# A transformer block on one core: the mixer's second stage reads the input and normalises it again, and some transfers and vector steps change their slots

## The chip, the cores and the metric

The kernel runs on one core of a Trainium2 chip. The core has a matrix engine (TensorE, PE in the profile; its weight loads are listed apart as PEld), a vector engine (VectorE, DVE), a scalar engine for functions such as the exponential (ScalarE, ACT), a general engine (GpSimd, POOL) and a sync engine (SyncE, SP), which here only issues transfers. Each engine runs its own instructions in its own order and waits for the others at semaphores. Transfers are issued by SP and POOL and carried out by 16 DMA engines. Matrix products are written to PSUM, which DVE and ACT can read; everything else lies in SBUF or in DRAM.

The metric is the device time of one execution in microseconds, and of several executions the median.

## The reference

All inputs are bfloat16. The sequence has 2048 tokens of 512 values.

```python
x  = A_x                                   # [1, 2048, 512]
xn = layernorm(x)                          # over the 512 values
# A: attention, 32 heads of 128, with given keys and values
q  = (xn @ A_wq) split into 32 heads
p  = softmax(q @ k_cache^T * 128 ** -0.5)  # 2048 x 2048 for each head
s  = concat(p @ v_cache) @ A_wo
# B: a mixer on the same xn, which it normalises once more
h  = gelu(layernorm(xn) @ B_w1)            # 512 x 512
hs = (h, its four quarters shifted by 1, -1, 2, -2 tokens) @ B_w2
x1 = xn + hs
h2 = gelu(layernorm(x1) @ B_w3) @ B_w4     # 512 x 1792, 1792 x 512
out = x + s * silu(x1 + h2)
```

The largest part of the work is attention: for each head 2048 x 2048 scores, their exponentials, and their product with the values.

## The kernel before

Attention is cut into 128 units. A unit is one head with a block of 512 query tokens; units run by groups of four heads, in a group by query block, in a block by head. A unit has 8 slots (`SPU`), so the main loop has 1024 slots; slot n is slot p = n % 8 of unit u = n // 8. In each slot PE multiplies two key chunks with the queries (`s_slot`, tile `ps_s`), and ACT takes the exponential of the 128x1024 result into `pT`. Five slots later (`LAG`) PE multiplies `pT` with the values (`pv_slot`, tile `ps_o`). DVE adds the exponentials up in `acc` (`add_first`, `add_next`, `add_last`), PE turns them into sums over the keys (`sums`, `ps_sum`, in slot 3 of the next unit), DVE takes the reciprocal `rc`, and SP sends it through DRAM (`dr`) to all partitions (`rb`). In slot 2 of the unit after that, `norm` multiplies `ps_o` by `rb` into `oT`, which frees one of the two `ps_o` buffers; the unit that comes two later writes into it from its slot 5.

The queries of unit u + 2 are made in slots 0 and 1 of unit u (`q_mm`, `ps_q`), from the transposed normalised input `xnT` and the head's weights, and copied by DVE in slot 2 (`q_copy`, `qT`). The first unit of each query block of the first group needs four new tiles of tokens in `xnT`: unit 4 (made in slots 22 and 23) tiles 4 to 7, unit 8 (slots 48 and 49) tiles 8 to 11, unit 12 (slots 80 and 81) tiles 12 to 15. The queries, the sums and the output projection share one PSUM tile by turns.

The output projection (`wo_mm`, `wo_post`) and the mixer (`chunks`: `m1_chunk`, `m2_chunk`, `m3_chunk`, `m4_chunk`, tiles `ps_m`) run as additional matrix work inside the slots, the mixer in slots 2, 3, 6 and 7 at an even density from unit 5 on. The mixer's second stage `m2_chunk(t)` works on token tile t: four products in `ps_m`, then `x1` on DVE, which adds the normalised input from the tile `xr` and so frees `ps_m`, then new statistics (`stats`). Since layernorm of an already normalised row is almost the same row, the mixer's first layernorm is the same `xn`.

The 2048 tokens are 16 tiles of 128. For each tile, `ln1_load` brings the input (`xin`), `ln1_stats` takes mean and variance on DVE (`bn`, `mv`) and the reciprocal root on POOL (`rsqrt`: `ve`, `rs`), `ln1_apply` normalises it on DVE into `xn`, has SP transpose it into `xnT` by a DMA, and has POOL write `xn` to DRAM (`xn_d`). The tiles 0 to 3 go another way (`first_tokens`, transposed by PE), but are written to `xn_d` too, in slots 9 to 12. `xn_load(t)` reads `xn_d` back for the mixer's second stage.

The order on each engine is the program order wherever `pin(...)` stands, and nearly everything is pinned. `at(n, fn)` puts a step behind the fixed work of slot n. SP and POOL issue their transfers one after the other, so that a transfer whose data are not ready holds up those behind it. For the token tiles 4 to 15 the slots of `ln1_stats` and `ln1_apply` are two lists in one loop; `ln1_load` of the tiles 8 to 15 comes 8 slots ahead of the statistics.

At the end, `tail_open` in unit 121 (`QUIET`) loads what the last four token tiles need, `gate_sum(t)` prepares their result on DVE with two operations on 128x512 tiles, in slot 4 of units 122 to 125, and behind the loop stands the drain: the last products of unit 127, its sums and reciprocal, `norm`, and the last projections.

Of the kernel before, what the change touches and what calls it, by code (L numbers as in the profile page):

```python
# [17 lines left out]
def kernel(  # L18
# [15 lines left out]
    nc = tc.nc  # L34
# [4 lines left out]
    Sq, D = x2d.shape  # L39
# [91 lines left out]
    def at(n, fn):  # L131
        todo[n].append(fn)
# [213 lines left out]
    def ln1_stats(t):  # L346
        xin = ln[t]
        bn = smp.tile([P, nc.vector.BN_STATS_DIM], FP32, name="bn")
        mv = smp.tile([P, nc.vector.BN_AGGR_DIM], FP32, name="mv")
        rs = smp.tile([P, 1], FP32, name="rs")  # L350
        pin(nc.vector.bn_stats(out=bn[:], in_=xin[:]))  # L351
        pin(nc.vector.bn_aggr(out=mv[:], in_=bn[:]))
        rsqrt(rs[:], mv[:, 1:2])
        ln[t] = (xin, mv, rs)

    def ln1_norm(t):
        xin, mv, rs = ln.pop(t)
        xn = tokp.tile([P, D], BF16, tag="tb", bufs=8, name="xn")
        pin(nc.vector.tensor_scalar(
            out=xn[:], in0=xin[:], scalar1=mv[:, 0:1], scalar2=rs[:],  # L360
            op0=ALU.subtract, op1=ALU.mult))
        return xn

    def ln1_apply(t):
        xn = ln1_norm(t)
        pin(nc.sync.dma_start_transpose(out=xnT[:, :, t * P:(t + 1) * P], in_=xn[:]))
        pin(nc.gpsimd.dma_start(out=xn_d[t][:], in_=xn[:]))

# [5 lines left out]
    def first_tokens():  # L374
# [453 lines left out]
```

## Time and profile before

| what | value |
|---|---|
| median of 3 executions | 1293.24 us |
| lowest, highest | 1289.54, 1295.29 us |
| the profiled execution, device time | 1290.41 us |
| its span, first to last instruction | 1288.6 us |
| PE, ACT, DVE, POOL busy | 1267.2, 1114.5, 1016.6, 146.0 us |
| PE's mean granted clock | 0.997 |
| DMA, mean over the span | 88 GB/s |

Lines of the timelines give the start, the length, the engine, the line of the kernel, the operation, the tile written and those read, and the count; in brackets stands how long the engine had been idle before it, and what the profile names as the releaser. PE's instructions all have line 115, the helper `mm`, so they are told apart by tile. SPq is SP's queue of transfers; its entries are the issue of a transfer, not its run. A row "DMA to landing" gives the least, the middle and the greatest time from the issue to the arrival of the data. Granted clock 1.00 is PE's full speed.

### The profile page before, as it was taken

Reading aid. Unit: us, or ns where it says so; the run is one execution under the profiler, and the core shown is the slowest. Engines: PE = TensorE matmul, PEld = TensorE weight load, DVE = VectorE, ACT = ScalarE, POOL = GpSimd, SP = SyncE. Lnnn points to the kernel's source line nnn. Section 1 sums busy time; section 2 is a strip of 40 time slices with the busy share of each in tenths; the row PEclk is TensorE's granted clock in tenths of the full one; section 3 lists DMA queues with packets and bytes.
Section 4 is the critical chain, followed back from the end, with each engine's and each line's share of the span. In section 5 each row is a group of like instructions: output and inputs, shape, how many; then the busy total and the mean of one; then the engine's idle time right before and its main releaser. Section 6 shows DMA issues by size and latency. Waiting matters only on the chain.

```text
span 1288.6 us, 17369 instructions
## 1 busy us (share of the span) xinstructions
PE 1267.2 (98%) x6320; PEld 612.3 (48%) x6320; DVE 1016.6 (79%) x1392; ACT 1114.5 (86%) x1195; POOL 146.0 (11%) x257
## 2 busy tenths in 40 slices
PE   8899999999999999999999999999999999999998
PEld 4444444444444444444444444444444444444443
DVE  6887788888788777778787777888777888777895
ACT  7788998888999988899998889998888999888983
POOL 5332002333111110000001000000000000000110
PEclk9999999999999999999999999999999999999999
DMA  9644353357433553234344234523635134452521
GB/s 185 148 96 104 70 89 84 80 121 153 103 74 79 98 112 82 58 74 79 71 91 89 58 78 84 100 51 66 100 73 99 33 68 73 90 107 54 138 68 54
DMA packets 173718, 113.89 MB, mean 88 GB/s; under 512 B 125056, under 2 KB 150144, under 8 KB 173632
## 3 DMA queue, kind: packets, MB, share of 16 engines
q1 hardware_dynamic: 163904, 85.51, 33.9%
q0 software_dynamic: 9440, 27.01, 8.3%
q8 instruction: 49, 0.80, 0.3%
q14 instruction: 37, 0.30, 0.1%
q10 hardware_dynamic: 288, 0.26, 0.1%
HBM read 82.58 MB, written 9.70 MB: 72 GB/s over the span
## 4 chain that ended last, share of the span: by engine, by line
PE 85%; ACT 7%; DVE 5%; DMA 1%; issue 1%; POOL 0%; DVEq 0%; SPq 0%; ACTq 0%; POOLq 0%
PE ps_s L115 31%; PE ps_o L115 29%; PE ps_m L115 9%; PE ps_wo L115 8%; PE ps_q L115 7%; ACT pT L195 5%; DVE acc L206 2%; PE ps_sum L115 1%; ACT sq L431 1%; DMA xin<-in_A_x_dram 1%; ACT pre L461 1%; DVE acc L211 1%; DMA vb<-in_A_v_cache_dram 0%; DVE bn L351 0%; DVE qT L181 0%
## 5 line engine op out<-in xcount | busy, mean ns | idle before, releaser
L195 ACT ACTIVATE pT<-ps_s 128x1024 bf16<-128x1024 f32 x1024 | 1013.4, 1030 | 148.9 <-PE ps_s L115 145.1
L115 PE MATMUL ps_s<-qT,kT 128*128 128x512 bf16 x2048 | 609.6, 379 | 2.0 <-ACT pT L195 0.7
L115 PE MATMUL ps_o<-pT,vb 128*128 128x512 bf16 x2048 | 609.1, 379 | 2.1 <-DVE oT L262 2.1
L206 DVE TENSOR_TENSOR acc<-acc,pT 128x2048 bf16<-128x2048 bf16 x254 | 309.9, 1220 | 59.8 <-ACT pT L195 54.2
L115 PEld LDWEIGHTS <-kT 128*128 128x128 bf16 x2048 | 226.9, 113 | 224.6 <-issue 19.1
L115 PEld LDWEIGHTS <-vb 128*128 128x128 bf16 x2048 | 200.0, 98 | 228.0 <-issue 3.4
L201 DVE TENSOR_TENSOR acc<-pT 128x2048 bf16<-128x2048 bf16 x128 | 155.8, 1217 | 30.9 <-ACT pT L195 30.7
L115 PE MATMUL ps_q<-xnT,wq_h 128*128 128x512 bf16 (+1 forms) x524 | 152.4, 375 | 5.5 <-DVE acc L211 2.6
L115 PE MATMUL ps_wo<-wo_h,oT 128*128 128x512 bf16 x468 | 138.8, 379 | 0.0
L329 DVE TENSOR_TENSOR s_acc<-ps_wo,s_acc 128x512 f32<-128x512 f32 x100 | 68.9, 689 | 81.8 <-PE ps_wo L115 81.8
L262 DVE TENSOR_TENSOR oT<-ps_o,rb 128x512 bf16<-128x512 f32 x129 | 87.2, 676 | 6.1 <-DMA rb<-dr 6.1
L211 DVE TENSOR_TENSOR acc<-acc 128x1024 bf16<-128x1024 bf16 x127 | 87.9, 692 | 4.3
L181 DVE CAST qT<-ps_q 128x512 bf16<-128x512 f32 x122 | 83.6, 685 | 9.7 <-PE ps_q L115 9.7
L115 PEld LDWEIGHTS <-wq_h 128*128 128x128 bf16 x524 | 50.6, 98 | 66.6 <-issue 6.4
L115 PEld LDWEIGHTS <-oT 128*128 128x128 bf16 x480 | 46.9, 98 | 57.7 <-issue 2.6
L115 PE MATMUL ps_m<-xn2T,w_sb 128*128 128x512 bf16 x224 | 66.5, 378 | 0.0
L115 PE MATMUL ps_m<-w_sb,h2T 128*128 128x512 bf16 x224 | 63.9, 378 | 0.0
L580 POOL DMA_DIRECT2D w_sb<-in_B_w_dram x28 | 21.1, 755 | 352.7 <-PE ps_m L115 317.2
L212 DVE TENSOR_TENSOR acc<-acc 128x512 bf16<-128x512 bf16 x127 | 54.0, 425 | 4.3
L115 PEld LDWEIGHTS <-acc 128*128 128x128 bf16 x516 | 37.0, 115 | 33.9 <-DVE acc L212 5.9
L234 DVE RECIPROCAL rc<-ps_sum 128x4 f32<-128x4 f32 x128 | 22.9, 179 | 37.1 <-PE ps_sum L115 36.1
L612 POOL DMA_DIRECT2D g_d<-xr x16 | 8.8, 548 | 345.3 <-DVE xr L610 345.3
(75 smaller groups left out, 604.1 us busy)
## 6 DMA issues: line engine op xcount, KB each, us to landing
rb<-dr SPq DMA_DIRECT2D x128, 256.0 KB, 4.4
vb<-in_A_v_cache_dram SPq DMA_DIRECT2D x64, 256.0 KB, 4.6
w_sb<-in_B_w_dram POOLq DMA_DIRECT2D x28, 256.0 KB, 4.2
wo_h<-in_A_wo_dram SPq DMA_DIRECT2D x32, 128.0 KB, 4.5
wq_h<-in_A_wq_dram SPq DMA_DIRECT2D x28, 128.0 KB, 4.8
kT<-in_A_k_cache_dram SPq DMA_TRANSPOSE x128, 4.7
xn_d<-xn POOLq DMA_DIRECT2D x16, 128.0 KB, 4.1
dr<-rc SPq DMA_DIRECT2D x128, 2.0 KB, 1.4
```

Of the source, the lines that this page charges most:

```text
L115: pin(nc.tensor.matmul(out=out, lhsT=lhsT, rhs=rhs, start=start, stop=stop))
L181: pin(nc.vector.tensor_copy(out=qT[:], in_=st[u].pop("psq")[:]))
L195: pin(nc.scalar.activation(out=s["pT"][-1][:, jj:jj + 2, :], in_=sps[:], func=ACT.Exp, scale=SCALE))
L201: pin(nc.vector.tensor_tensor(out=s["acc"][:], in0=s["pT"][0][:], in1=s["pT"][1][:], op=ALU.add))
L206: pin(nc.vector.tensor_tensor(out=a[:], in0=a[:], in1=st[u]["pT"][i][:], op=ALU.add))
L211: pin(nc.vector.tensor_tensor(out=a[:, 0:2, :], in0=a[:, 0:2, :], in1=a[:, 2:4, :], op=ALU.add))
L212: pin(nc.vector.tensor_tensor(out=a[:, 0, :], in0=a[:, 0, :], in1=a[:, 1, :], op=ALU.add))
L234: pin(nc.vector.reciprocal(out=rc[:], in_=ps[:]))
L262: pin(nc.vector.tensor_tensor(out=oTs[(g, qt)][:, hh, c], in0=s["o"][:, c], in1=s["rb"][:, c], op=ALU.mult))
L329: pin(nc.vector.tensor_tensor(out=sa, in0=ps[:], in1=sa, op=ALU.add))
L431: pin(nc.scalar.activation(out=sq[:], in_=pre[:], func=ACT.Square, scale=GELU_A ** 0.5))
L580: pin(nc.gpsimd.dma_start(out=w[:], in_=w3_v[:, :, fc * P:(fc + 2) * P]))
```

## The change

- The normalised input is no longer kept in DRAM: `xn_d`, its 16 writes by POOL and the four steps in slots 9 to 12 are gone. `xn_load(t)` reads the raw input of tile t instead, and a new step `norm1` on DVE normalises it in place, one slot ahead of `x1`: in slot 3 for a piece that starts in slot 2, in slot 6 for one that starts in slot 6. Mean and reciprocal root of each tile therefore stay in SBUF (`mv1`, `rs1`) in place of turning buffers.
- `ln1_apply` is cut in two: normalising (`ln1_apply`) and the transposing transfer (`ln1_turn`), each with its slot. The tiles 4 and 5 keep the slots of their statistics and normalising, and their transposes go one and two slots later; tiles 6 and 7 stay. The tiles 8 to 15 move earlier: their normalising was in slots 29, 37, 45, 47, 53, 61, 69, 77 and is in slots 23, 29, 31, 37, 45, 53, 61, 69. Loads stay 8 slots ahead of the statistics.
- The first half of head 2's values is loaded in slot 7 in place of slot 11.
- `gate_sum` of the tiles 12 and 13 stands in units 122 and 124; those of 14 and 15 stand in the drain, behind `bcast` of the last unit.

PE and ACT have the same instructions in the same order in both kernels. DVE has 16 more, POOL 16 fewer, SP the same number.

```diff
-    xn_d = [dsp.tile([P, D], BF16, name=f"xn_d{t}") for t in range(NT)]
...
     def ln1_stats(t):
         xin = ln[t]
         bn = smp.tile([P, nc.vector.BN_STATS_DIM], FP32, name="bn")
-        mv = smp.tile([P, nc.vector.BN_AGGR_DIM], FP32, name="mv")
-        rs = smp.tile([P, 1], FP32, name="rs")
         pin(nc.vector.bn_stats(out=bn[:], in_=xin[:]))
-        pin(nc.vector.bn_aggr(out=mv[:], in_=bn[:]))
-        rsqrt(rs[:], mv[:, 1:2])
-        ln[t] = (xin, mv, rs)
+        pin(nc.vector.bn_aggr(out=mv1[t][:], in_=bn[:]))
+        rsqrt(rs1[t][:], mv1[t][:, 1:2])
+
+    def norm1(t, out, in_):
+        pin(nc.vector.tensor_scalar(
+            out=out, in0=in_, scalar1=mv1[t][:, 0:1], scalar2=rs1[t][:],
+            op0=ALU.subtract, op1=ALU.mult))
...
     def ln1_apply(t):
-        xn = ln1_norm(t)
-        pin(nc.sync.dma_start_transpose(out=xnT[:, :, t * P:(t + 1) * P], in_=xn[:]))
-        pin(nc.gpsimd.dma_start(out=xn_d[t][:], in_=xn[:]))
+        xns[t] = ln1_norm(t)
+
+    def ln1_turn(t):
+        pin(nc.sync.dma_start_transpose(out=xnT[:, :, t * P:(t + 1) * P], in_=xns.pop(t)[:]))
...
-        for t in range(4):
-            at(9 + t, lambda t=t: pin(nc.gpsimd.dma_start(out=xn_d[t][:], in_=xns[t][:])))
...
     def xn_load(t):
         mlp["xnext"] = tokp.tile([P, D], BF16, tag="tb", bufs=8, name="xr")
-        nc.gpsimd.dma_start(out=mlp["xnext"][:], in_=xn_d[t][:])
+        nc.gpsimd.dma_start(out=mlp["xnext"][:], in_=xsrc[t])
...
             if i == 0:
                 mlp["ps"] = psX.tile([P, 512], FP32, tag="xm", name="ps_m")
-                mlp["xr"] = mlp.pop("xnext")
+                xr = mlp["xr"] = mlp.pop("xnext")
+                at(n + 1 if n % SPU == 2 else n, lambda: norm1(t, xr[:], xr[:]))
...
-    for t, stats, apply in zip(range(4, NT), (2, 5, 8, 11, 23, 31, 39, 39, 47, 55, 63, 71),
-                               (4, 9, 12, 14, 29, 37, 45, 47, 53, 61, 69, 77)):
+    tokens = ((2, 4, 5), (5, 9, 11), (8, 12, 12), (11, 14, 14),
+              (21, 23, 23), (23, 29, 29), (29, 31, 31), (31, 37, 37),
+              (39, 45, 45), (47, 53, 53), (55, 61, 61), (63, 69, 69))
+    for t, (stats, apply, turn) in enumerate(tokens, 4):
         if t >= 8:
             at(stats - 8, lambda t=t: ln1_load(t, nc.gpsimd))
         at(stats, lambda t=t: ln1_stats(t))
         at(apply, lambda t=t: ln1_apply(t))
+        at(turn, lambda t=t: ln1_turn(t))
...
-    for n, h, half in ((11, 2, 0), (13, 2, 1), (19, 3, 0), (20, 3, 1)):
+    for n, h, half in ((7, 2, 0), (13, 2, 1), (19, 3, 0), (20, 3, 1)):
         at(n, lambda h=h, half=half: load_v(h, (half,)))
...
     for t in range(4 * LQ, NT):
-        at((QUIET + 1 + t % 4) * SPU + 4, lambda t=t: gate_sum(t))
+        if t % 4 < 2:
+            at((QUIET + 1 + 2 * (t % 4)) * SPU + 4, lambda t=t: gate_sum(t))
...
     bcast(U)
+    for t in ts[2:]:
+        gate_sum(t)
     pv_slot(U, 6)
```

More of the change, by code (lines that the diff above doesn't have):

```diff
@@ L348, in ln1_stats @@
         bn = smp.tile([P, nc.vector.BN_STATS_DIM], FP32, name="bn")
-        mv = smp.tile([P, nc.vector.BN_AGGR_DIM], FP32, name="mv")
-        rs = smp.tile([P, 1], FP32, name="rs")
         pin(nc.vector.bn_stats(out=bn[:], in_=xin[:]))
-        pin(nc.vector.bn_aggr(out=mv[:], in_=bn[:]))
-        rsqrt(rs[:], mv[:, 1:2])
-        ln[t] = (xin, mv, rs)
+        pin(nc.vector.bn_aggr(out=mv1[t][:], in_=bn[:]))
[4 more added lines that the diff above has]
+            op0=ALU.subtract, op1=ALU.mult))
     def ln1_norm(t):
-        xin, mv, rs = ln.pop(t)
+        xin = ln.pop(t)
         xn = tokp.tile([P, D], BF16, tag="tb", bufs=8, name="xn")
-        pin(nc.vector.tensor_scalar(
-            out=xn[:], in0=xin[:], scalar1=mv[:, 0:1], scalar2=rs[:],
-            op0=ALU.subtract, op1=ALU.mult))
+        norm1(t, xn[:], xin[:])
         return xn
+    xns = {}
     def ln1_apply(t):
-        xn = ln1_norm(t)
-        pin(nc.sync.dma_start_transpose(out=xnT[:, :, t * P:(t + 1) * P], in_=xn[:]))
-        pin(nc.gpsimd.dma_start(out=xn_d[t][:], in_=xn[:]))
+        xns[t] = ln1_norm(t)
+    def ln1_turn(t):
+        pin(nc.sync.dma_start_transpose(out=xnT[:, :, t * P:(t + 1) * P], in_=xns.pop(t)[:]))
     def warm_up(n):
@@ L470 @@
     hT = ph1.tile([P, DC, Sq + PADW], BF16, name="hT")
+    mv1 = [ph1.tile([P, nc.vector.BN_AGGR_DIM], FP32, name=f"mv1_{t}") for t in range(NT)]
+    rs1 = [ph1.tile([P, 1], FP32, name=f"rs1_{t}") for t in range(NT)]
     def ph1_load():
```

## The prediction

> **What bounds the kernel now.** I read the page's busy shares, PE's list of waits, PE's timeline at those waits, then SP's queue and the landing times of the tile waited for.
>
> ```profile
> PE 1267.2 (98%) x6320; PEld 612.3 (48%) x6320; DVE 1016.6 (79%) x1392; ACT 1114.5 (86%) x1195; POOL 146.0 (11%) x257
> ```
> ```profile
> PE ps_q L115 <- DVE acc L211: 2.6, 1, 2.6
> ...
> PE ps_q L115 <- DVE acc L212: 2.0, 1, 2.0
> ```
>
> PE is the bound, and its instructions do not change, so only its stalls can move the end. PE's timeline places the long ones, all ahead of 115 us; the two windows give the clock behind the longest (granted clock is the number ahead of DMA share and GB/s).
>
> ```profile
> 33.95 0.59 PE L115 MATMUL ps_o<-pT,vb 128*128 128x512 bf16 x2 [2.13 <-DVE oT L262]
> 34.38 0.59 PE L115 MATMUL ps_s<-qT,kT 128*128 128x512 bf16 x2
> ...
> 36.19 0.59 PE L115 MATMUL ps_q<-xnT,wq_h 128*128 128x512 bf16 x2 [0.78 <-DMA vb<-in_A_v_cache_dram]
> ...
> 59.85 0.27 PE L115 MATMUL ps_sum<-ones_t,acc 128*128 128x1 bf16 x4 [0.68 <-DVE qT L181]
> ...
> 68.60 0.59 PE L115 MATMUL ps_q<-xnT,wq_h 128*128 128x512 bf16 x2 [1.99 <-DVE acc L212]
> ...
> 102.21 0.27 PE L115 MATMUL ps_sum<-ones_t,acc 128*128 128x1 bf16 x4 [0.29 <-DVE qT L181]
> ...
> 110.94 0.74 PE L115 MATMUL ps_q<-xnT,wq_h 128*128 128x512 bf16 x2 [2.61 <-DVE acc L211]
> ```
> ```profile
> 111.00:113.00 2.00, 2.00 (x6) 0.76 (x7) 0.06 (x1) 0.43 (x1) 0.54 (x1) 0.56 0.56 182
> 113.00:115.00 2.00, 2.00 (x6) 0.70 (x5) 0.72 (x2) 0.61 (x2) 0.00 (x0) 0.58 0.04 14
> ```
>
> A pair's record lasts 0.59, but pairs start 0.43 apart (33.95, 34.38), so a true gap is 0.16 longer than its bracket: 2.29, 0.94, 0.84, 2.15, 0.45 and 2.77. At 0.56 and 0.58 of the clock, four microseconds lose 2 x 0.44 + 2 x 0.42 = 1.72 more.
>
> The profile names DVE for the waits of 1.99 and 2.61. I take them for late transposes of `xnT`. SP's queue shows the issues; the three landing rows are those of `xnT` in the windows 25 to 40, 60 to 72 and 100 to 113 us:
>
> ```profile
> 24.53 0.52 SPq L236 DMA_DIRECT2D dr<-rc  x1
> ...
> 26.34 0.58 SPq L157 DMA_DIRECT2D vb<-in_A_v_cache_dram  x1
> 27.78 0.34 SPq L251 DMA_DIRECT2D rb<-dr  x1
> ...
> 30.18 1.21 SPq L366 DMA_TRANSPOSE xnT<-xn  x1
> ...
> 62.79 3.77 SPq L366 DMA_TRANSPOSE xnT<-xn  x2
> ...
> 104.74 1.22 SPq L366 DMA_TRANSPOSE xnT<-xn  x1
> ```
> ```profile
> DMA to landing us min/median/max: 5.9/6.3/6.7
> ```
> ```profile
> DMA to landing us min/median/max: 3.1/3.8/4.5
> ```
> ```profile
> DMA to landing us min/median/max: 6.1/6.1/6.1
> ```
>
> Tile 15: issued 104.74, landed 6.1 later at 110.84; PE goes on at 110.94. Tile 7: 30.18 + 5.9 = 36.08; PE at 36.19. Tile 11, the second of the pair at 62.79, ends its issue at 66.56, so starts near 65.4, and with 3.1 lands at 68.5; PE at 68.60. All three agree to 0.1 us.
>
> **The change part by part: the ramp.** The rows that carry prices, from DVE and POOL, and the landing row of `xin` after 20 us:
>
> ```profile
> 23.11 0.17 DVE L234 RECIPROCAL rc<-ps_sum 128x4 f32<-128x4 f32 x1
> ...
> 33.21 0.69 DVE L262 TENSOR_TENSOR oT<-ps_o,rb 128x512 bf16<-128x512 f32 x1 [3.06 <-DMA rb<-dr]
> ...
> 45.30 1.23 DVE L206 TENSOR_TENSOR acc<-acc,pT 128x2048 bf16<-128x2048 bf16 x1 [0.59 <-ACT pT L195]
> ...
> 55.20 0.69 DVE L351 BATCH_NORM_STATS2 bn<-xin 128x6 f32<-128x512 bf16 x1 [0.65 <-DMA xin<-in_A_x_dram]
> ```
> ```profile
> L359 DVE TENSOR_SCALAR xn<-xin,mv,rs x16: 380/406/427, 6.9 to 103.9; 128x512 bf16<-128x512 bf16 x16
> ```
> ```profile
> 47.44 1.10 POOL L119 TENSOR_SCALAR ve<-mv 128x1 f32<-128x1 f32 x1 [1.88 <-DVE mv L352]
> 48.63 0.99 POOL L120 TENSOR_TENSOR rs<-ve,nhalf 128x1 f32<-128x1 f32 x1
> ```
> ```profile
> DMA to landing us min/median/max: 2.3/2.9/5.9
> ```
>
> Unit 2 (gaps 2.29 and 0.94). `rc` is done at 23.28, but `dr` goes out at 24.53, behind the transpose of tile 5. That transpose now follows `dr`: 1.2 earlier. `rb` waits for `dr`, and the values' issue of 0.58 at 26.34 leaves the queue (slot 7), so `rb` and the transpose of tile 7 start 1.2 to 1.4 earlier. The values now pass ahead of `dr` while `rc` is not ready, which costs nothing. The transposes of tiles 4 and 5, passed by a key piece, the values and `dr`, go out about 1 us later; tile 5's, near 24, lands by 31 even with the slowest 6.7, ahead of tile 7's, so they cost nothing unless slot 22 comes before that. Of `xn_d` eight writes (a tile each) leave this stretch and two loads (tiles 8, 9) enter; landing took 5.9 here against 3.1 to 4.5 later, so I add 0.6. Gain 1.9; ends: the issue alone, 1.2, and both gaps, 3.2.
>
> Unit 3 pays. In slots 24 to 31 DVE had one normalisation and one set of statistics and now has two of each: 0.41 + 0.69 more. Tile 10 is normalised two slots behind its statistics; POOL's pair takes 1.10 + 0.99, an add of 1.23 lies between, so DVE waits 0.86. Its idle 0.59 at 45.30 covers a part: 1.10 + 0.86 - 0.59 = 1.4 lost. Ends: 0.5 with no wait for POOL, 2.0 with no cover.
>
> Unit 4 (0.84): slot 39 had two sets of statistics and waited 0.65 for `xin`; it now has one, so its chain is 1.3 shorter. The load is again issued behind a set of statistics 8 slots earlier and may be waited for again. Gain 0.8; ends 0.2 and 0.84.
>
> Unit 5 (2.15): tile 11's transpose moves from slot 47 to 37, needed in 48; even the slowest landing quoted, 6.7, fits. Gain 2.15. Late next is DVE's own add chain, which the bracket names; it loses one normalisation too. Ends 1.0 (the sums of slot 51 wait instead) and 2.15.
>
> Unit 8 (0.45): the statistics in slot 71, 0.69, are gone. Gain 0.45; ends 0 and 0.45.
>
> Unit 9: tile 15's transpose moves from slot 77 to 69, needed in 80. Gain 2.77, and the half clock's 1.72. Ends 2.0 and 4.5. On the clock, the Trainium skill, page "TensorE: Matmul & The Clock Gate", section "Part 1: The HAM clock gate", says that the array falls back to half its clock after about 3.4 us of idle window. Here a gap of 2.77 was followed by a clock of 0.56, while behind the gap of 2.29 the pairs ran at full rate at once (33.95, 34.38); the trace so puts the limit between the two, lower than the page. By the page's figure the drop would have another cause than this gap, the 1.72 would stay, and the sum would end at 1285.2 (as in rival C).
>
> POOL's issues of `xn_d` go too; nothing on PE's path waits for them apart from what is counted. The eight early loads of `xr` now follow tile 15's statistics (slot 63), away from its needed landing.
>
> **The mixer's second stage.** Sixteen `norm1` of 0.41 enter DVE between 200 and 325 us.
>
> ```profile
> 240.00:280.00 40.00, 40.00 (x201) 19.43 (x200) 34.51 (x55) 32.76 (x33) 12.53 (x23) 1.00 0.43 93
> ```
> ```profile
> 225.56 0.18 DVE L234 RECIPROCAL rc<-ps_sum 128x4 f32<-128x4 f32 x1 [0.57 <-PE ps_sum L115]
> 226.08 1.23 DVE L201 TENSOR_TENSOR acc<-pT 128x2048 bf16<-128x2048 bf16 x1 [0.34 <-ACT pT L195]
> ...
> 250.45 0.69 DVE L509 SCALAR_TENSOR_TENSOR xr<-ps_m,xr 128x512 bf16<-128x512 f32 x1 [0.77 <-PE ps_m L115]
> ```
>
> DVE is busy 34.5 of 40 us there, PE all of it. Where the piece starts in slot 6, `norm1` falls into the 0.77 in which DVE waits for PE; where it starts in slot 2, the unit has 0.57 + 0.34 of idle behind PE and ACT. Queued behind `norm1` are `add_first` and `x1`; PE waits for `x1` only two slots later. Cost 0; ends 0 and 16 x 0.41 = 6.5 if no cover held.
>
> **The end.**
>
> ```profile
> 1238.62 1.23 DVE L201 TENSOR_TENSOR acc<-pT 128x2048 bf16<-128x2048 bf16 x1 [0.81 <-ACT pT L195]
> 1239.77 0.68 DVE L300 SCALAR_TENSOR_TENSOR s_acc<-s_acc,gf 128x512 f32<-128x512 f32 x1
> ...
> 1250.48 0.69 DVE L329 TENSOR_TENSOR s_acc<-ps_wo,s_acc 128x512 f32<-128x512 f32 x1 [0.53 <-PE ps_wo L115]
> ...
> 1273.58 0.18 DVE L234 RECIPROCAL rc<-ps_sum 128x4 f32<-128x4 f32 x1 [0.95 <-PE ps_sum L115]
> 1276.19 0.69 DVE L329 TENSOR_TENSOR s_acc<-ps_wo,s_acc 128x512 f32<-128x512 f32 x1 [2.43 <-PE ps_wo L115]
> ...
> 1279.49 0.76 DVE L262 TENSOR_TENSOR oT<-ps_o,rb 128x256 bf16<-128x256 f32 x2 [1.43 <-DMA rb<-dr]
> ```
>
> Unit 125 loses its step, but DVE waits 0.53 for PE behind it: no gain. Unit 124 keeps one (tile 13's), and DVE enters it idle for 0.81, so unit 123's relief is not handed on: no gain. In the drain four operations of 0.68 make 2.7; DVE idles 2.43 there, and the 0.3 left over disappears in the 1.43 before `rb`. Cost 0; ends: gain 1, loss 0.3 if `rb` came at once.
>
> **Sum:** -1.9 + 1.4 - 0.8 - 2.15 - 0.45 - 4.5 = -8.4. The profiled execution, 1290.41 (span 1288.6 and 1.8 around it, which stay), gives 1282.0. The three timed ones have their median 2.8 above it; the mean of all four is 1292.1, which gives 1283.7. I take 1283.5, 9.7 below the median shown.
>
> **Rivals.**
> B. `norm1` is not covered: 6.5 back, 1290. For it: DVE has little idle in units with two pieces; against: the brackets.
> C. The half clock stays or falls behind another gap: 1.7 back, 1285.2. For it: what counts as a long enough gap hangs on one case; against: no gap above 1.5 is expected.
> D. Unit 2 gains all and unit 3 loses nothing: 1.3 + 1.4 more, 1281.
> E. Slower: the loop statistics, POOL pair, next `xin`, statistics (2.1 + up to 5.9 = 8.0 us, against 8 slots) falls behind in units 3 to 6; DVE and then PE stop long enough to lose the clock too, 2.77 + 1.72 = 4.5 for each of tiles 10 to 13. Two such gaps use up the gain, four give 1301.5. For it: 0.65 was waited for already; against: a gap of this size needs a landing near 10 us, and 5.9 is the longest.
> F. The transposes are issued earlier but the waits stay, since DVE was the cause as the brackets say: 1292. Against: the three landings above.
>
> **How the numbers follow.** A measurement of this kernel tells 0.5%, 6.5 us, from no change: faster is below 1286.8, slower above 1299.7. Chances: the forecast 0.58 (its own range 1279 to 1287), B 0.14, C 0.10, D 0.06, E 0.10, F 0.02. Faster 0.56 + 0.07 (C) + 0.06 = 0.69; slower 0.05 (half of E); the rest, 0.26, same. The range 1277.5 to 1290.5 reaches from D in a quick execution (1281 less 2.6, the distance of the quickest run from the mean, and 1 at the end) to B; it leaves out E, F and B's upper part.
>
> **What would show it.** Right: no bracket above 1.5 on `ps_q` up to 115 us, no window with a clock below 0.9 there, a stall of about 1 us at the sums near 50 us, PE busy 40.00 in the second stage's windows, the same brackets after 1220. Wrong: waits of DVE for `xin` or `rs` above 2 us before 70 us, `ps_sum` or `ps_m` waiting for DVE between 200 and 330 us, or the stalls of 1.99 and 2.61 still there with the transposes landed.

## The result and the profile after

The changed kernel takes 1282.11 us in the median (four executions, 1281.89 to 1282.37), the kernel before 1293.97 us beside it (four, 1289.54 to 1295.29). The ratio is 0.9914, 95% interval 0.989 to 0.9939: faster by 0.9%, and by more than the 0.5% that a measurement can tell. The profiled execution takes 1282.06 us with a span of 1280.3, against 1290.41 and 1288.6 before: 8.3 us less, the 8.4 of the forecast's sum within 0.1. The kernel before spreads over 6 us, the changed one over half a microsecond; in three later comparisons on three chips before has medians of 1288.43, 1289.61 and 1289.56, so the ratio moves with the kernel before by about 0.4%. A later run of the changed kernel gave 0.9938 (0.9923 to 0.9952), with 1281.79. One of the four executions of `even` (below) ran at a mean clock of 0.752, took 1643.55 us and is left out of its ratio.

The busy shares of the changed kernel's page, and its list of what PE waited for (total, times, longest):

```profile
PE 1258.8 (98%) x6195; PEld 612.5 (48%) x6320; DVE 1021.5 (80%) x1408; ACT 1113.4 (87%) x1195; POOL 139.2 (11%) x241
```
```profile
PE ps_sum L114 <- DVE qT L180: 2.2, 2, 1.7
PE ps_sum L114 <- DVE acc L211: 1.7, 4, 0.5
...
PE ps_o L114 <- DVE oT L261: 0.4, 1, 0.4
```

No wait of a product with the queries (`ps_q`) is left in the list; before, two of 2.6 and 2.0 stood there. The 125 matmuls that PE's count lacks are records missing from this trace, not work. DVE does 16 operations more and is busy 4.9 us longer.

PE's timeline of the changed kernel, the sums of the first units (one row ends each unit) and one product with the values; a number in brackets is an idle time ahead of the row. Between 22 and 1220 us PE has only three brackets more, 0.17, 0.17 and 0.40 at 443, 880 and 1094 us, waits for ACT:

```profile
22.36 0.27 PE L114 MATMUL ps_sum<-ones_t,acc 128*128 128x1 bf16 x4
29.69 0.27 PE L114 MATMUL ps_sum<-ones_t,acc 128*128 128x1 bf16 x4
39.46 0.27 PE L114 MATMUL ps_sum<-ones_t,acc 128*128 128x1 bf16 x4 [0.50 <-DVE qT L180]
41.41 0.59 PE L114 MATMUL ps_o<-pT,vb 128*128 128x512 bf16 x2 [0.36 <-DVE oT L261]
49.76 0.26 PE L114 MATMUL ps_sum<-ones_t,acc 128*128 128x1 bf16 x4 [1.72 <-DVE qT L180]
...
108.03 0.27 PE L114 MATMUL ps_sum<-ones_t,acc 128*128 128x1 bf16 x4
```

The distance from one sum to the next is the time of a unit. The sums are in slot 3 of the next unit, so "unit 2" is the time from the sum in slot 19 to that in slot 27.

| unit | before | after | measured | the sum's term |
|---|---|---|---|---|
| 1 | 7.97 | 7.33 | -0.64 | none |
| 2 | 12.36 | 9.77 | -2.6 | -1.9 |
| 3 | 7.98 | 10.30 | +2.3 | +1.4 |
| 4 | 9.30 | 8.42 | -0.9 | -0.8 |
| 5 | 12.20 | 10.27 | -1.9 | -2.15 |
| 8 | 10.28 | 9.84 | -0.45 | -0.45 |
| 9 | 14.30 | 9.83 | -4.5 | -4.5 |

Units 6 and 7 agree within 0.03; the rows add up to about 8.6 us less, and the first sum comes 0.1 later than before. Behind unit 9 nothing moves: from the sum at 108.03 on, everything comes about 8.3 to 8.5 us earlier than before, and the brackets of 0.53, 0.53, 0.31 and 0.31 at the last four long sums stand at 1220.10, 1238.37, 1247.76 and 1257.16 as they did at 1228.40, 1246.67, 1256.07 and 1265.46. The row of the windows for the mixer's second stage (PE, PEld, DVE, ACT, POOL busy; granted clock; DMA):

```profile
240.00:280.00 40.00, 39.79 (x196) 19.43 (x199) 36.81 (x62) 32.73 (x33) 11.76 (x21) 1.00 0.58 118
```

DVE went from 34.51 to 36.81 there, and no bracket of PE appeared (PE has 196 records there for 201 before; the 0.21 that its sum lacks goes with the missing ones). The price of `norm1` was 0, as forecast.

Unit 9, where the clock had fallen to 0.56, in the changed kernel:

```profile
105.00:107.00 2.00, 2.00 (x11) 0.95 (x10) 1.93 (x4) 2.00 (x4) 0.00 (x0) 1.00 0.00 0
...
113.00:115.00 2.00, 2.00 (x11) 0.97 (x10) 1.04 (x2) 1.83 (x3) 0.00 (x0) 1.00 1.06 142
```

And three idle times of DVE between 22 and 50 us; the last two are in the stretch of unit 3:

```profile
30.10 0.69 DVE L261 TENSOR_TENSOR oT<-ps_o,rb 128x512 bf16<-128x512 f32 x1 [0.72 <-DMA rb<-dr]
...
40.66 0.69 DVE L261 TENSOR_TENSOR oT<-ps_o,rb 128x512 bf16<-128x512 f32 x1 [1.26 <-DMA rb<-dr]
...
45.58 0.41 DVE L353 TENSOR_SCALAR xn<-xin,mv,rs 128x512 bf16<-128x512 bf16 x1 [0.77 <-POOL rs L119]
```

The wait for `rs` is the 0.86 of the forecast; the one of 1.26 for `rb` was not in it.

### The profile page after: what moved, and what is told of

It is laid out like the page before. It is cut to its first block, busy times and chain, and to the rows that moved or that the text cites. A ratio compares the mean times of both kernels' runs of the same rounds, so it can differ in the third digit from the quotient of the medians.

```text
span 1280.3 us, 17229 instructions
## 1 busy us (share of the span) xinstructions
PE 1258.8 (98%) x6195; PEld 612.5 (48%) x6320; DVE 1021.5 (80%) x1408; ACT 1113.4 (87%) x1195; POOL 139.2 (11%) x241
## 4 chain that ended last, share of the span: by engine, by line
PE 85%; ACT 6%; DVE 5%; issue 2%; DMA 1%; SPq 0%; POOL 0%; DVEq 0%; ACTq 0%
PE ps_s L114 31%; PE ps_o L114 29%; PE ps_m L114 9%; PE ps_wo L114 8%; PE ps_q L114 7%; ACT pT L194 4%; DVE acc L205 2%; PE ps_sum L114 1%; ACT sq L431 1%; DMA rb<-dr 1%; ACT pre L461 1%; DVE acc L210 0%; DVE bn L348 0%; DVE gl L332 0%; DVE acc L200 0%
## 5 line engine op out<-in xcount | busy, mean ns | idle before, releaser
L114 PE MATMUL ps_s<-qT,kT 128*128 128x512 bf16 x2004 | 599.4, 379 | 4.1 <-ACT pT L194 1.0
L114 PE MATMUL ps_o<-pT,vb 128*128 128x512 bf16 x1997 | 597.6, 379 | 3.2 <-DVE oT L261 0.4
L205 DVE TENSOR_TENSOR acc<-acc,pT 128x2048 bf16<-128x2048 bf16 x254 | 309.9, 1220 | 59.6 <-ACT pT L194 53.9
L114 PE MATMUL ps_wo<-wo_h,oT 128*128 128x512 bf16 x456 | 136.2, 379 | 0.6
```

Source lines behind the costliest of these rows:

```text
L114: pin(nc.tensor.matmul(out=out, lhsT=lhsT, rhs=rhs, start=start, stop=stop))
L205: pin(nc.vector.tensor_tensor(out=a[:], in0=a[:], in1=st[u]["pT"][i][:], op=ALU.add))
```

## The experiments

Theory: the time is in the stalls of units 2 to 9; the slots of the transposes take the stalls of units 5, 8 and 9 away, an earlier place in SP's queue most of unit 2's, and unit 3 pays with DVE work. Rivals: the missing transfers to and from `xn_d` do it all, whatever the slots; or POOL's issues do.

### Before once more, and each half of the change alone

`before_again` is the kernel before, unchanged, for a second trace.

> The kernel before, once more, for the spread of its executions (1289.5 to 1295.3, where the changed kernel has 1281.9 to 1282.4). Theory 1: the length of the gaps near 34, 68 and 111 us is alike in all, and the slow executions lose 1.7 us each time PE's clock also falls to half behind the gap of 2.3 or of 2.2; a trace at 1290 shows one drop, one at 1294 or above two or three. Theory 2: the transposes land later in some executions and the gaps themselves differ by microseconds; then the clock has one drop in any trace.

`slots_only` is the kernel before with the slots of the changed one for tokens and values; the tiles are written to `xn_d` and read back, and the gate steps stand as before. Against the kernel before:

```diff
-        xn = ln1_norm(t)
-        pin(nc.sync.dma_start_transpose(out=xnT[:, :, t * P:(t + 1) * P], in_=xn[:]))
-        pin(nc.gpsimd.dma_start(out=xn_d[t][:], in_=xn[:]))
+        xns[t] = ln1_norm(t)
+        pin(nc.gpsimd.dma_start(out=xn_d[t][:], in_=xns[t][:]))
+
+    def ln1_turn(t):
+        pin(nc.sync.dma_start_transpose(out=xnT[:, :, t * P:(t + 1) * P], in_=xns.pop(t)[:]))
...
+    tokens = ((2, 4, 5), (5, 9, 11), (8, 12, 12), (11, 14, 14),
+              (21, 23, 23), (23, 29, 29), (29, 31, 31), (31, 37, 37),
+              (39, 45, 45), (47, 53, 53), (55, 61, 61), (63, 69, 69))
...
-    for n, h, half in ((11, 2, 0), (13, 2, 1), (19, 3, 0), (20, 3, 1)):
+    for n, h, half in ((7, 2, 0), (13, 2, 1), (19, 3, 0), (20, 3, 1)):
```

> The kernel before with the changed slots of tokens, transposes and values alone; xn_d is still written and read back, no norm1, gate steps as before. Theory (late transposes were the waits): the gaps near 68 and 111 us and the half clock are gone (2.15 + 2.77 + 1.72 = 6.6), the unit-1 gain of 0.6 is missing and unit 2 gains less: 1283 to 1285. Rival (POOL's writes made the transposes late): most of the gain is missing, 1288 or more.

`dram_only` is the changed kernel with the old slots for tokens and values:

```diff
-    tokens = ((2, 4, 5), (5, 9, 11), (8, 12, 12), (11, 14, 14),
-              (21, 23, 23), (23, 29, 29), (29, 31, 31), (31, 37, 37),
-              (39, 45, 45), (47, 53, 53), (55, 61, 61), (63, 69, 69))
+    tokens = ((2, 4, 4), (5, 9, 9), (8, 12, 12), (11, 14, 14),
+              (23, 29, 29), (31, 37, 37), (39, 45, 45), (39, 47, 47),
+              (47, 53, 53), (55, 61, 61), (63, 69, 69), (71, 77, 77))
...
-    for n, h, half in ((7, 2, 0), (13, 2, 1), (19, 3, 0), (20, 3, 1)):
+    for n, h, half in ((11, 2, 0), (13, 2, 1), (19, 3, 0), (20, 3, 1)):
```

> The changed kernel with the old slots of tokens, transposes and values: only the DRAM copy is gone, with norm1 in the second stage and the gate steps as changed. Theory: unit 1 gains 0.6 (the reciprocal root of tile 7 comes earlier from POOL), unit 2 up to 1, the gaps near 68 and 111 us stay with the half clock: 1 to 2 us below the kernel before of the same rounds. Rival (the writes' traffic made the transposes late): gaps near 68 and 111 us shrink to under 1 us and most of the gain is there, 1284.

Measured: before 1288.43 us on this chip (1286.76 to 1292.87); `before_again` 1287.94; `slots_only` 1283.32, ratio 0.9951 (0.9932 to 0.9971); `dram_only` 1283.37, ratio 0.9952 (0.9934 to 0.997). Each half alone brings 5.1 us, both together some 6.5 (the changed kernel takes 1281.8 to 1282.1): they do not add up, because both take time out of units 4, 5 and 9 by different means. `slots_only` is where its theory put it, 1283 to 1285. `dram_only` missed both its values: 1 to 2 us were expected, and its gaps near 64 and 105 us are neither the old ones nor under 1 us (1.40 and 1.66, with the clock at 1.00). The units tell which (same measure as above):

| unit | before | before_again | slots_only | dram_only | after |
|---|---|---|---|---|---|
| 1 | 7.97 | 7.97 | 7.97 | 7.33 | 7.33 |
| 2 | 12.36 | 12.77 | 12.16 | 10.02 | 9.77 |
| 3 | 7.98 | 7.98 | 8.96 | 7.99 | 10.30 |
| 4 | 9.30 | 8.98 | 8.42 | 8.55 | 8.42 |
| 5 | 12.20 | 12.29 | 10.27 | 11.46 | 10.27 |
| 8 | 10.28 | 10.29 | 9.84 | 10.29 | 9.84 |
| 9 | 14.30 | 11.88 | 9.83 | 11.50 | 9.83 |

Unit 8 follows the slots, as the theory said, and unit 5 in the main: without the writes alone it is 0.7 shorter, with the slots 1.9. Unit 2 does not: with the slots and the queue order of the changed kernel, but with the writes, it still takes 12.16. PE's timeline and SP's queue of `slots_only`, and the landing row of its tiles 6 and 7 (window 27 to 32 us):

```profile
35.52 0.60 PE L115 MATMUL ps_q<-xnT,wq_h 128*128 128x512 bf16 x2 [2.54 <-DMA xnT<-xn]
```
```profile
23.17 0.34 SPq L236 DMA_DIRECT2D dr<-rc  x1
...
26.16 0.52 SPq L251 DMA_DIRECT2D rb<-dr  x1
...
28.71 1.21 SPq L371 DMA_TRANSPOSE xnT<-xn  x1
```
```profile
DMA to landing us min/median/max: 4.4/5.6/6.8
```

The transpose of tile 7 goes out 1.5 us earlier than before's 30.18 and takes 6.8 us instead of 5.9: of what the queue gained, the landing takes back 0.9, and at the next sums PE waits 0.3 longer for DVE (0.50 against 0.18). In the changed kernel the same two land in 3.8 and 3.9 us:

```profile
DMA to landing us min/median/max: 3.8/3.8/3.9
```

In `dram_only`, with the old order of the queue, it is:

```profile
DMA to landing us min/median/max: 3.7/3.9/4.1
```

So it was the writes to `xn_d` that held unit 2, not the order of SP's queue.

Unit 9 differs between the two traces of the same kernel before, 14.30 and 11.88. PE's timeline of `before_again`:

```profile
110.03 0.59 PE L115 MATMUL ps_q<-xnT,wq_h 128*128 128x512 bf16 x2 [1.88 <-DVE acc L206]
```

With 0.16 for the length of a pair's record that gap is 2.04, and 9.83 + 2.04 = 11.87 is the unit. In the first trace 9.83 + 2.77 + 1.72 = 14.32. The clock is 1.00 behind the shorter gap. So before's own spread is in part this: a landing of 5.4 or 6.1, and with it the fall of the clock or not. Neither expectation holds whole: the gaps differ by 0.7 us, not by microseconds, and this trace has no fall of the clock at all; an execution near 1294 was not traced.

### POOL's issues without the traffic

`tiny_writes` puts POOL's sixteen issues back, but each writes 8 KB that nobody reads in place of 128 KB:

```diff
     def ln1_apply(t):
         xns[t] = ln1_norm(t)
+        pin(nc.gpsimd.dma_start(out=tiny[t][:], in_=xns[t][:, 0:32]))
...
+        for t in range(4):
+            at(9 + t, lambda t=t: pin(nc.gpsimd.dma_start(out=tiny[t][:], in_=xns[t][:, 0:32])))
```

> The changed kernel, and at the sixteen places where the kernel before wrote a normalised tile to DRAM, POOL issues a write of its first 32 columns (8 KB instead of 128 KB) to a spare DRAM tile that nobody reads; the result is the same. POOL's issues are back, the traffic is not. Theory (the traffic of the writes stretched the transposes' landings in unit 2; the issues on POOL's queue alone only delayed the 1/sigma of tile 7 and with it unit 1 by 0.64 us): 1282.4 us, unit 2 takes 9.8 to 10.2 us, landings of tiles 4 to 7 no longer than 4.5 us. Rival (POOL's issues, in whose queue the statistics of the next tile stand, held unit 2): unit 2 takes 12 us or more and the time is 1284.5 to 1285.5.

Measured: 1281.74 us (1281.72 to 1282.71), ratio 0.9945 (0.993 to 0.996). Units 1 to 3 take 7.97, 10.39 and 8.95. The rows are PE's timeline, POOL's queue ahead of the 1/sigma of tile 7, DVE behind it, and the landings of tiles 6 and 7:

```profile
30.99 0.29 PE L115 MATMUL ps_sum<-ones_t,acc 128*128 128x1 bf16 x4 [0.47 <-DVE acc L212]
34.66 0.61 PE L115 MATMUL ps_q<-xnT,wq_h 128*128 128x512 bf16 x2 [0.76 <-DMA xnT<-xn]
41.38 0.27 PE L115 MATMUL ps_sum<-ones_t,acc 128*128 128x1 bf16 x4 [0.50 <-DVE qT L181]
```
```profile
25.81 1.13 POOL L425 DMA_DIRECT2D tiny<-xn  x2
26.97 0.55 POOL L119 TENSOR_SCALAR ve<-mv 128x1 f32<-128x1 f32 x1
27.59 0.57 POOL L120 TENSOR_TENSOR rs<-ve,nhalf 128x1 f32<-128x1 f32 x1
```
```profile
28.20 0.41 DVE L354 TENSOR_SCALAR xn<-xin,mv,rs 128x512 bf16<-128x512 bf16 x1 [0.77 <-POOL rs L120]
```
```profile
DMA to landing us min/median/max: 3.6/4.3/5.0
```

The issues cost unit 1 its 0.64 again: the 1/sigma of tile 7 stands behind four of them, DVE waits 0.77 for it, and the sums in slot 19 wait for DVE. Unit 2 is 0.6 longer than in the changed kernel's first trace and a little beyond the theory's 10.2, as the landing of 5.0 is beyond its 4.5. How much of this the issues cost is open: in six traces with the changed kernel's slots and no writes unit 2 takes 9.68 to 10.01 us, and in `even` (below) 10.27. The 1.8 between this run and `slots_only`, which has the same slots and issues but the large writes, are traffic. The rival, 12 us and more, falls. The end is not moved at all, though units 1 and 2 are 1.3 us longer: unit 3 is 1.35 shorter, since DVE does not wait for `rb` there (see the last experiment).

### Tile 15's transpose late

`turn15_77` is the changed kernel with the transpose of tile 15 issued in slot 77 as before, `turn15_79` in slot 79:

```diff
-              (39, 45, 45), (47, 53, 53), (55, 61, 61), (63, 69, 69))
+              (39, 45, 45), (47, 53, 53), (55, 61, 61), (63, 69, 77))
```

> The changed kernel, but tile 15's transpose is issued in slot 77 as before; its statistics and normalising on DVE stay in slots 63 and 69. Late transpose: the gap of about 2.7 at ps_q near 102 us comes back, and with it the half clock: 1286.6. DVE's add chain, as the profile's bracket named it: nothing comes back, 1282. A gap without the clock's fall (the Trainium skill's page TensorE: Matmul & The Clock Gate puts the idle window at about 3.4 us): 1284.9.

> The changed kernel with the transpose of tile 15 issued in slot 79 instead of 73, two slots later than in the kernel before; nothing is written to DRAM, so the landing should stay near 4.2 us as in the run with slot 77, where PE's gap was 0.68 us. Two slots are 2.5 us: a gap of 3.0 to 3.4 us in unit 9. Theory A (a gap of this length brings the clock down behind it, as the 2.77 us one in the kernel before did): 1282.1 + 3.2 + 1.7 = 1287, clock near 0.56 in the 4 us behind the gap. Theory B (the clock fall needs more than the one gap, such as the row of gaps of 1 to 3 us from 33 to 105 us in the kernel before): 1285.3 and clock 1.00 behind it. The landing may also come out at 2.5 to 3 us when little else moves, the gap then 1.5 to 2 us, 1283.8.

Measured: 1282.29 (1281.87 to 1282.4) and 1282.72 us (1282.64 to 1283.22), unit 9 10.68 and 10.95. Both expectations missed. I had taken slot 77 for the cause of the 4.5 us; alone it costs 0.85. And slot 79 is no later than slot 77. SP's queue and PE's timeline of `turn15_79`, with the landing row of tile 15:

```profile
98.29 0.33 SPq L235 DMA_DIRECT2D dr<-rc  x1
99.73 0.33 SPq L250 DMA_DIRECT2D rb<-dr  x1
100.11 1.22 SPq L369 DMA_TRANSPOSE xnT<-xn  x1
```
```profile
104.84 0.59 PE L114 MATMUL ps_q<-xnT,wq_h 128*128 128x512 bf16 x2 [0.95 <-DMA xnT<-xn]
```
```profile
DMA to landing us min/median/max: 4.5/4.5/4.5
```

In either slot the transpose stands behind `dr` and `rb` of the last unit, and `rb` waits 1.4 us for `dr` to land. Slot 77 gave an issue at 99.89. So this pair did not make a longer gap and tells nothing of the clock. What it tells is the make-up of unit 9. Counted from the sum of unit 8, the issue came 2.5 us later in both traces of before, 2.3 in these two, and 4.0 in `dram_only`; the landing took 6.1 and 5.4, 4.2 and 4.5, and 3.5. Issue plus landing is 8.6, 7.9, 6.5, 6.8 and 7.5 us, and PE's gaps (bracket and 0.16) are 2.77, 2.04, 0.84, 1.11 and 1.66: everywhere the gap is what goes beyond 5.7 to 5.9 us. Before, six reads of `xr` were issued right behind the write of tile 15 itself, while the transpose was on its way (POOL's timeline of the kernel before):

```profile
104.58 0.55 POOL L367 DMA_DIRECT2D xn_d<-xn  x1 [2.46 <-DVE xn L359]
105.13 3.19 POOL L493 DMA_DIRECT2D xr<-xn_d  x6
```

The long landing goes with these transfers in both traces of before, but taking them away alone at that place was not tried: `dram_only` issues seven reads of the raw input 1 to 5 us ahead of its transpose, and its `dr` took 2.9 us to land.

### Is the second stage free?

`norm_x3` normalises each of the 16 tiles twice more into a spare tile that nobody reads, so DVE gets 32 more operations in the stage:

```diff
-                at(n + 1 if n % SPU == 2 else n, lambda: norm1(t, xr[:], xr[:]))
+                def norms():
+                    for _ in range(2):
+                        norm1(t, spare[:], xr[:])
+                    norm1(t, xr[:], xr[:])
+                at(n + 1 if n % SPU == 2 else n, norms)
```

> The changed kernel with two more normalising operations of the same size beside each of the 16 in the second stage, into a tile that nobody reads: 32 x 0.33 to 0.41 = 10.6 to 13 us more DVE work between 190 and 325 us. Theory (cover of about 1 us for each piece is left): cost 0 to 3 us. Rival (DVE was at its limit with one): 10 us or more.

Measured: 1287.37 us (1286.8 to 1287.52), 5.6 above the changed kernel of the same comparison (`after_again`, 1281.79). The windows' row of the stage, the brackets of its sums, and DVE's group of the added operations:

```profile
240.00:280.00 40.00, 38.29 (x188) 18.32 (x187) 38.38 (x66) 31.50 (x32) 13.31 (x24) 1.00 0.51 113
```
```profile
197.84 0.27 PE L114 MATMUL ps_sum<-ones_t,acc 128*128 128x1 bf16 x4 [0.85 <-DVE qT L180]
...
228.80 0.27 PE L114 MATMUL ps_sum<-ones_t,acc 128*128 128x1 bf16 x4 [0.93 <-DVE qT L180]
...
279.98 0.27 PE L114 MATMUL ps_sum<-ones_t,acc 128*128 128x1 bf16 x4 [1.51 <-DVE qT L180]
```
```profile
L353 DVE TENSOR_SCALAR spare<-xr,mv,rs 128x512 bf16<-128x512 bf16 x32 | 13.2, 411 | 0.6
```

From the sums near 187 us to the fifteenth sums behind them the changed kernel takes 147.3 us and this one 152.9. Both expectations, at most 3 and at least 10, missed. The 13.2 us of work cost 5.6: the idle time of DVE in the stage covers 16 operations wholly and of 32 more about 7.6 us. The cover was there, and it is nearly used up, with DVE at 38.4 of 40.

### The small parts, and the changed kernel again

`gates_back` has all four gate steps in units 122 to 125; `v_back` loads the first half of head 2's values in slot 11; `after_again` is the changed kernel.

```diff
-        if t % 4 < 2:
-            at((QUIET + 1 + 2 * (t % 4)) * SPU + 4, lambda t=t: gate_sum(t))
+        at((QUIET + 1 + t % 4) * SPU + 4, lambda t=t: gate_sum(t))
...
-    for t in ts[2:]:
-        gate_sum(t)
```

> The changed kernel with all four gate sums of the last tiles back in units 122 and 124, none in the drain. Theory (the drain's four gate steps hide between the last rc and the last oT, which waits for the broadcast of rb for 1.36 us anyway, and DVE has room in units 122 to 125): within 0.3 us of the changed kernel, 1281.8 to 1282.4. Rival (the two steps moved into the drain sit on the path to the end): 1281.0 to 1281.5. Other rival (the four steps in the units held PE's sums there): 1282.8 or more, with longer brackets than 0.53 at the last four sums.

```diff
-    for n, h, half in ((7, 2, 0), (13, 2, 1), (19, 3, 0), (20, 3, 1)):
+    for n, h, half in ((11, 2, 0), (13, 2, 1), (19, 3, 0), (20, 3, 1)):
```

> The changed kernel with the first half of head 2's values read in slot 11 again instead of slot 7. Theory (nothing of unit 1 or 2 waits for it, values of head 2 are first used in unit 8 or later): within 0.4 us of the changed kernel, 1281.7 to 1282.5. Rival (the read in slot 11 stands in SP's queue ahead of the transposes of tiles 4 to 7 and its 256 KB stretches their landing): unit 2 0.5 to 1.5 us longer, 1282.6 to 1283.6.

> The changed kernel once more, beside the kernel before and the next three on one chip. The first comparison gave 0.9914; on the chip of the four runs above the kernel before is 5 us faster, without the fall of the clock. Theory (the kernel before varies with the landing of its transposes, the changed one does not wait for them): 1282 again on any chip, and the ratio follows the kernel before alone. Rival (the chip as a whole is faster): 1277.

Measured: 1281.67 us (1281.38 to 1283.01), 1281.97 (1281.85 to 1282.52) and 1281.79 (1281.49 to 1282.11). Neither part is worth anything that can be measured in the time, and the changed kernel itself came out as its theory said, not at the rival's 1277. Unit 2 of `v_back` is 10.27 us, 0.5 longer as the rival had it, but `even` (below), which has the load in slot 7, shows the same 10.27, and the transposes of tiles 6 and 7 land in 3.6 and 3.9 us, no later than in the changed kernel. The drain, DVE's timeline of `gates_back` and then of the changed kernel:

```profile
1264.96 0.18 DVE L233 RECIPROCAL rc<-ps_sum 128x4 f32<-128x4 f32 x1 [1.01 <-PE ps_sum L114]
1267.57 0.69 DVE L328 TENSOR_TENSOR s_acc<-ps_wo,s_acc 128x512 f32<-128x512 f32 x1 [2.43 <-PE ps_wo L114]
...
1270.89 0.76 DVE L261 TENSOR_TENSOR oT<-ps_o,rb 128x256 bf16<-128x256 f32 x2 [1.44 <-DMA rb<-dr]
```
```profile
1265.28 0.18 DVE L233 RECIPROCAL rc<-ps_sum 128x4 f32<-128x4 f32 x1 [1.01 <-PE ps_sum L114]
1265.38 0.66 DVE L299 SCALAR_TENSOR_TENSOR s_acc<-s_acc,gf 128x512 f32<-128x512 f32 x1
...
1268.01 0.68 DVE L328 TENSOR_TENSOR s_acc<-ps_wo,s_acc 128x512 f32<-128x512 f32 x1
...
1271.24 0.76 DVE L261 TENSOR_TENSOR oT<-ps_o,rb 128x256 bf16<-128x256 f32 x2 [1.36 <-DMA rb<-dr]
```

From `rc` to `oT` it is 5.93 us without the four operations and 5.96 with them: they fill DVE's 2.43 of idle, and the rest comes out of the wait for `rb`.

### A version that pays less in unit 3

If DVE's work in unit 3 costs the 2.3 us, spreading the tokens must give them back. `even` has one set of statistics and one normalisation in each unit from 3 on; `even_rb` has besides the last key pieces and values of head 3 one to two slots later, so that fewer transfers run beside `rb`:

```diff
-              (21, 23, 23), (23, 29, 29), (29, 31, 31), (31, 37, 37),
-              (39, 45, 45), (47, 53, 53), (55, 61, 61), (63, 69, 69))
+              (21, 23, 23), (23, 29, 29), (29, 33, 33), (37, 41, 41),
+              (45, 49, 49), (53, 57, 57), (61, 65, 65), (69, 72, 72))
...
-    for n, h, piece in ((2, 2, 2), (4, 2, 3), (11, 3, 0), (15, 3, 1), (17, 3, 2), (19, 3, 3)):
+    for n, h, piece in ((2, 2, 2), (4, 2, 3), (11, 3, 0), (15, 3, 1), (19, 3, 2), (21, 3, 3)):
...
-    for n, h, half in ((7, 2, 0), (13, 2, 1), (19, 3, 0), (20, 3, 1)):
+    for n, h, half in ((7, 2, 0), (13, 2, 1), (20, 3, 0), (22, 3, 1)):
```

> The changed kernel with the token steps of tiles 10 to 15 spread so that from slot 24 on each unit holds one normalisation and one set of statistics, two or more slots apart: tile 10 (29, 33, 33), 11 (37, 41, 41), 12 (45, 49, 49), 13 (53, 57, 57), 14 (61, 65, 65), 15 (69, 72, 72) for statistics, normalising, transpose. Theory (unit 3 loses 2.3 us because DVE has 1.1 us more work there and waits 0.8 for POOL): the stall of 1.7 at the sums near 49 us is gone, units 4 to 8 stay as they are, about 1.7 faster than the changed kernel. Rival (unit 3 is held by norm waiting 1.3 for rb): the stall shrinks by half at most, 0.5 to 0.9 faster. If tile 15's transpose comes too late, a gap of up to 1 near 100 us takes some back.

> As even, and the last key pieces and the values of head 3 go out one to two slots later (pieces in slots 19 and 21 in place of 17 and 19, values in 20 and 22 in place of 19 and 20), behind dr and rb of unit 1. Theory (rb of unit 1 is late because it queues behind them): norm waits less than 0.5 for rb near 40 us, and 0 to 0.6 us are gained over even. Rival (not on the path once DVE has less work): same as even.

Measured: `even` 1279.82, 1281.39 and 1281.80 us, ratio 0.9936 (0.9916 to 0.9956); `even_rb` 1279.61 (1279.23 to 1279.98), ratio 0.9921 (0.9906 to 0.9935). Unit 3 is 8.03 and 7.99 us, the 7.98 of before: without the extra steps nothing is left of the 2.3. That does not make all 2.3 DVE's work. The start of `oT` in `tiny_writes`, to set beside the row at 40.66 of the changed kernel, which waited 1.26 for `rb`:

```profile
41.24 0.68 DVE L262 TENSOR_TENSOR oT<-ps_o,rb 128x512 bf16<-128x512 f32 x1
```

There `oT` does not wait. From its start to the sums that end unit 3 it is 9.09 us (41.24 to 50.33), and in the changed kernel 9.10 (40.66 to 49.76); in all nine traces with these slots it is 9.09 or 9.10, and DVE's only idle time in that stretch is the 0.77 or 0.78 for `rs`. So a late `rb` is passed on in full. With `oT` on time unit 3 takes 8.95 and 8.96 (`tiny_writes`, `slots_only`); in the seven others it takes 9.76 to 10.30, and 10.30 is the trace shown. About 1.0 of the 2.3 is thus DVE's steps with the wait for `rs`, and 1.3 (in the other traces 0.8 and more) is `rb`, for which DVE has no idle time left. In `even` `rb` still took 5.1 us to land, and `oT` began 0.39 after the sums, but unit 3 is only 0.05 longer than before's; what a lateness of 1.2 would cost without the steps no run shows. In `even_rb` `oT` does not wait for `rb`, as its theory said. PE's timeline of `even_rb`, the end of units 2 and 3:

```profile
39.05 0.27 PE L114 MATMUL ps_sum<-ones_t,acc 128*128 128x1 bf16 x4 [0.50 <-DVE qT L180]
47.04 0.27 PE L114 MATMUL ps_sum<-ones_t,acc 128*128 128x1 bf16 x4
```

The stall of 1.72 is gone. `even_rb` is 2.2 us faster than the changed kernel beside it (1279.23 to 1279.98 against 1281.49 to 1282.11) and the fastest here. For `even` the traced execution, 1279.82, shows the gain and the two others hardly do; where they lost it no trace shows. So the spreading alone is not shown to give more than about 0.4 us in the median, nor is the rest shown to come from the later transfers.

## Why the prediction was right, point by point

The forecast was 1283.5 us, with 1277.5 to 1290.5 as its range and 0.69 for faster; it came out at 1282.1, and the sum against the profiled execution at 8.4 for a measured 8.3. The mechanism was right in the main: stalls of PE ahead of 115 us go, most of them by earlier transposes, and nothing is lost later. That 8.4 met 8.3 is luck: units 1 and 2 gave 1.3 us more than the sum has, units 3 and 5 1.1 less, and one term was right for half the reason.

- **What bounds it: right.** PE's stalls up to 115 us, and in them the transposes of `xnT` though the profile names DVE: with earlier slots those stalls are gone while DVE has more work. Rival F falls with them.
- **Unit 2: the size was short, and the split of it wrong.** The step that failed is "the issue alone, 1.2" with "so I add 0.6" for the writes. `slots_only` has the earlier issue and gains 0.2 (12.16 against 12.36); `dram_only` has no writes and the old order and gains 2.3. The writes were the term, and the order of the queue next to nothing while they ran. The landing of 5.9 to 6.7 that I quoted and set against 3.1 to 4.5 elsewhere was the sign of it: the middle values, 6.3 and 3.8, differ by 2.5, and most of that should have gone into the term; the 6.1 of tile 15 belonged with the long ones.
- **"POOL's issues of `xn_d` go too; nothing on PE's path waits for them": wrong, by 0.64.** They stood ahead of the 1/sigma of tile 7; with small writes in their place unit 1 takes 7.97 again.
- **Unit 3: the right place, mis-sized, 1.4 for 2.3.** The two more operations and the wait for `rs` (0.77 for 0.86) came as said; by themselves they cost 1.0 (8.95 and 8.96 where `oT` does not wait). What the term put at nothing is `rb`: it was issued at 35.3 and landed 5.4 us later, DVE stood 1.26 before `oT`, and the unit takes 1.3 more than with `oT` on time. Without the extra steps (`even`) the unit is back at 8.03.
- **Units 4, 5 and 8: right** (0.9, 1.9 and 0.45 for 0.8, 2.15 and 0.45). In units 5 and 8 the slots do it, with or without the writes (10.27 and 9.84 in both). In units 4 and 5 `dram_only` gets 8.55 and 11.46 with the old slots, so taking away the writes would have done part of it too.
- **Unit 9: the size right, 4.5, the reason half.** The transpose was waited for and the clock fell behind the wait, and an earlier slot removes both. But the late slot costs only 0.85 by itself; the rest needed the long landing and the clock. In the second trace of before the same slot costs 2.04 and the clock does not fall.
- **The mixer's second stage, 0: right**, and rival B with its 6.5 out. `norm_x3` shows how near it was: of the next 13.2 us of such work, 5.6 come through.
- **The end, 0: right**, by the very rows: 2.43 filled, the rest in the wait for `rb`.
- **Rivals C, D, E.** C did not come up: no window is below 1.00 and no gap above 1.72 + 0.16 is left. D was right that unit 2 gains more, and wrong on unit 3. E's loop did fall behind once, in unit 3, by one wait for `rs`, not for `xin`, and without the clock.
- **What would show it:** all but one point held. A stall of about 1 us at the sums near 50 us was 1.72; the two brackets of 0.50 and 0.36 ahead of it were not named. PE's 39.79 in the second stage's window stands for 40.00, by the missing records.

The base is where the ratio is weak: before took 1293.97 us beside the changed kernel and some 1289 later. The sum taken off the profiled execution gave 1282.0, off the mean of the four times 1283.7; the first came nearer. A likely reason is that what the longer executions of before lose more, they lose in the stalls that the change takes away; none of them was traced.

## What to carry to other kernels

A transfer that nobody waits for is not free when it runs beside one that somebody waits for: look at the landing times of the waited-for transfer in stretches with and without the other traffic, before counting the order of the issuing queue. A step moved to a later slot is later only if the queue lets it: behind a transfer that waits for data two slots are one place. And when a change that moves work into a stretch wins elsewhere, look at what that stretch loses: spreading the same steps one per unit, with `rb` issued earlier, gave 2.2 us more. Here DVE, with no idle time left in that unit, passed a late `rb` on in full.

## What the runs showed of the hardware

- **Landing of a transpose.** The same 128x512 transpose from SBUF to SBUF, issued in 1.2 us, landed after 2.4 to 6.8 us, and the other traffic moved it. The slower of tiles 6 and 7 took 6.5 to 6.8 us in the three traces with seven writes of 128 KB between 24 and 34 us, 5.0 with seven of 8 KB, 3.8 to 4.1 in nine traces with none and 4.8 in a tenth (`even`); the 5.0 is hardly beyond that spread. The issues of that window in the kernel before and in `tiny_writes` (size of each, middle time to landing):

```profile
xn_d<-xn POOLq DMA_DIRECT2D x7, 128.0 KB, 4.4
```
```profile
tiny<-xn POOLq DMA_DIRECT2D x7, 8.0 KB, 2.4
```

  The Trainium skill, page "DMA: Bandwidth & Descriptors", section "Issuing engines are not separate DMA queues", says that transfers from the sync and the GpSimd engine end up on the same 16 DMA engines and interleave. The traces agree: with POOL's large writes SP's transposes took 6.5 to 6.8 us, without them 3.8 to 4.8.
- **The clock.** A gap of 2.77 us was followed by a granted clock of 0.56 and 0.58 for four microseconds; one of 2.70 (2.54 and 0.16) was not. Windows of `slots_only` around its gap:

```profile
34.00:36.00 2.00, 0.48 (x3) 0.27 (x4) 1.15 (x2) 0.00 (x0) 1.79 (x3) 1.00 1.23 191
36.00:38.00 2.00, 1.95 (x10) 0.99 (x10) 0.55 (x1) 1.14 (x2) 0.47 (x1) 1.00 0.81 197
```

  Nor was one of 2.29 or 2.04. Either the limit lies between 2.70 and 2.77, or the length is not all. The Trainium skill, page "TensorE: Matmul & The Clock Gate", section "Part 1: The HAM clock gate", has an idle window of about 3.4 us that runs freely, so that where in it a gap falls would count too. Its length is not confirmed here, since 2.77 was enough once; whether the place in a window decides, no run here shows.
- **The spread of the kernel before.** Of 45 timed executions of it on the later chips, 21 have a mean granted clock of 0.999 or 1.000 and take 1286.76 to 1290.24 us; 10 have 0.995 or 0.996 and take 1290.25 to 1292.87. The changed kernel's eight are all at 0.999 or 1.000. So lost clock goes with the slow end of before's spread, and a kernel without the long gaps is also steadier; in which gaps those executions lost it is not traced, beyond the one shown.
- **Small operations on POOL.** The 128x1 `ve` and `rs` took 1.10 and 0.99 us in the rows of the kernel before that the prediction shows, and 0.55 and 0.57 in the rows of `tiny_writes` above. What slows them was not tried.
